# Expert weights asked for later in a spectral-mixing and top-k expert kernel

## The chip, the cores and the metric

The kernel runs on one core of one Trainium2 chip, as one launch. The metric is the device time of an execution in microseconds; the time before is 379.39 us, the median of three runs (379.3 to 380.17). All arithmetic is in float32, apart from small whole numbers in bfloat16.

## The reference

```python
# x (8, 2496, 256), filt_r, filt_i (1249, 256)
X = np.fft.rfft(x, axis=1)
y = np.fft.irfft(X * (filt_r + 1j * filt_i)[None], n=2496, axis=1)     # gfnet mixing
# y as x (19968, 256); w_gate (256, 8), w1 (8, 256, 1024), w2 (8, 1024, 256), capacity 80
logits = x @ w_gate
expert_idx = np.argmax(logits, axis=1)
gate_w = softmax(logits)[np.arange(N), expert_idx]
out = np.zeros((N, D))
for e in range(8):
    tok_idx = np.where(expert_idx == e)[0]
    if len(tok_idx) > capacity:                 # the 80 tokens with the largest gate_w
        tok_idx = tok_idx[np.argpartition(-gate_w[tok_idx], capacity)[:capacity]]
    h = np.maximum(x[tok_idx] @ w1[e], 0.0)
    out[tok_idx] = gate_w[tok_idx, None] * (h @ w2[e])
```

So of 19968 mixed tokens only 640 (80 for each of 8 experts) go through an expert. All other rows of the output are zero.

## The kernel before, in words

The forward transform and the filter are done for all 8 batches as small matrix products (80 steps of the main loop, up to about 238 us). The result stays in the frequency domain: per batch a "page" of 128 x 5120 numbers, written to the DRAM tensors `yf` (the last batch stays in SBUF as `yt`). Gate values of all tokens come from a narrow inverse transform, and VectorE picks the 80 tokens for each expert by thresholds.

Only the rows of picked tokens are transformed back. For that the rows of the inverse transform's table that belong to the picked tokens are gathered by GpSimd (`gather_rows`, an indirect DMA into `gt`), turned by VectorE (`turn_rows`, into `wt`), and multiplied with the batch's page on TensorE (`fill(n)`: the next n of 20 steps of a round). There are 7 rounds of 128 rows, in the code 0 to 6 and in this text first to seventh or last. The first four rounds take one batch each; the last three take four groups of 32 rows from batches 4 to 7. At a round's end ScalarE copies the result into `yr` (one buffer; the sixth round's goes into `z`), and SyncE writes it to the DRAM tensor `y_sel`.

Then come the experts (`experts`). For each, 80 rows of `y_sel` are gathered by GpSimd with an indirect DMA, turned on TensorE (`turn`, tile `px`), and go through two layers (`layer1`, tile `ph`; `layer2`, tile `po`). Results are scattered to the output. The first two experts' rows, `xg_first`, are gathered from the first six rounds alone, and the last round's share is added on TensorE straight from `yr`. The gathers `xg_True` of the other six read all of `y_sel`, so they wait for the last row write too. On TensorE the order is: turn 0 and 1, layer 1 of the first and the second expert, layer 2 of the first with the turn of the third expert in its middle, layer 1 of the third, and so on.

An expert's weights are 2 MB, asked for by `load_weights(e)` as two DMAs of 1 MB each from SyncE's queue into a tile of 128 x 4096. Eight experts share five places: an own buffer (`weights`), and four buffers of pages, once the page's last reader is through. Which expert gets which place is the table `WT`. The order of everything here is that of the code (a manual schedule): each engine works off its instructions in the order of the program, and an instruction of SyncE that waits for a buffer keeps back all the later ones. SyncE's DMAs use eight completion counters in turn, so that each waits for the DMA eight places before it.

Of the kernel before, what the change touches and what calls it, by code (L numbers as in the profile page):

```python
# [13 lines left out]
F32 = mybir.dt.float32  # L14
# [5 lines left out]
B, S, C = 8, 2496, 256  # L20
# [13 lines left out]
E, FF = 8, 1024  # L34
NDB, NFC = C // 128, FF // 128
# [3 lines left out]
NH = 2  # L39
# [58 lines left out]
def kernel(  # L98
# [11 lines left out]
    nc = tc.nc  # L110
# [148 lines left out]
    with tc.manual_schedule():  # L259
        keep = pool("keep", 1)  # L260
        late = pool("late", 1)
        sp = pool("pick", 1)
        gt_p = pool("gt", 4)
        u_p = pool("u", 2)
# [565 lines left out]
        def load_page(b, where, tag="page", mark=None, eng=nc.sync):  # L830
            pages[b] = where.tile([128, NS * C], F32, name=f"page_{b}", tag=tag)
            if mark is not None:
                mark(pages[b][:, 0:1], 0.0)
            flat = yf[b].rearrange("p k i s w -> p (k i s w)")
            m = NS * C // 4
            for i in range(4):
                eng.dma_start(out=pages[b][:, m * i:m * i + m], in_=flat[:, m * i:m * i + m])
# [27 lines left out]
        where = {u: (r, c) for r, us in enumerate(ROUNDS) for c, u in enumerate(us)}  # L865

        def fill(n):
            for _ in range(n):
                r, s = todo.pop(0)
                if s == 0:  # L870
                    st["po"] = fps.tile([128, C], F32, name=f"pr_{r}", tag="f")
                w = 128 if r < EARLY else 32
                for c in range(0, 128, w):
                    b = ROUNDS[r][c // 32][0]
                    nc.tensor.matmul(st["po"][c:c + w, :], lhsT=wts[r][:, s, c:c + w],  # L875
                                     rhs=yt_t[:, :, s] if b == B - 1 else columns(pages[b], s), start=(s == 0),
                                     stop=(s == NS - 1))
                if s == NS - 1:
                    yr = (zs[:].rearrange("p e s -> p (e s)") if r == NR - 2 else
                          yr_p.tile([128, C], F32, name=f"yr_{r}", tag="yr"))  # L880
                    nc.scalar.copy(out=yr[:], in_=st["po"][:])  # L881
                    nc.sync.dma_start(
                        out=y_sel[128 * r:128 * r + 128, :], in_=yr[:])
                    st["yr"] = yr
# [6 lines left out]
        for g in range(NG):  # L891
            filter_in(g)
            nc.sync.dma_start(out=d_t[:, 4 * g:4 * g + 4, :],
                              in_=d_dram.ap()[:, 4 * g:4 * g + 4, :])
# [102 lines left out]
        for k in range(NK):  # L997
# [35 lines left out]
            if 75 <= k < 79:  # L1033
                nc.scalar.copy(out=st["u1"][:, k - 75],
                               in_=zero_t[:, 0:1].unsqueeze(2).to_broadcast([128, NS, 32]))
# [8 lines left out]
        def turn_all(r, units=None):  # L1044
            for b, g in ROUNDS[r][slice(*units) if units else slice(None)]:
                turn_rows(b, g)

        for name in ("t2", "pr", "fwd"):
# [6 lines left out]
        ones_f = near_p.tile([cap, 128], F32, name="ones_f")  # L1055
        nc.vector.memset(ones_f[:], 1.0)
        WT = [(w_p, "w"), (last, "page"), (late, "page0"), (pg_p, "page"), (late, "page1"),
              (w_p, "w"), (last, "page"), (late, "page0")]
        ws = {}

        def load_weights(e):
            where, tag = WT[e]
            ws[e] = where.tile([128, NDB * FF + NFC * C], F32, name=f"w_{e}", tag=tag)
            nc.sync.dma_start(out=ws[e][:, 0:NDB * FF].rearrange("p (k f) -> p k f", k=NDB),
                              in_=moe_w1[e].rearrange("(k p) f -> p k f", p=128))
            nc.sync.dma_start(out=ws[e][:, NDB * FF:].rearrange("p (k d) -> p k d", k=NFC),
                              in_=moe_w2[e].rearrange("(k p) d -> p k d", p=128))

        load_page(2, late, "page1", nc.vector.memset)
        load_page(3, last)  # L1070
        load_weights(0)
        for g in range(3):
            t = gt2_p.tile([128, NS, 32], F32, name=f"gt_z_{g}", tag="gt")
            nc.gpsimd.memset(t[:], 0.0)
# [32 lines left out]
        kept, rcnt, cnt = mark(B)  # L1107
        fill(13)
        load_page(5, pg_p)
        load_weights(1)  # L1110
        turn_last(7)
        turn_last(8)
        st["poff"] = poff = ranks(B, cnt)
# [11 lines left out]
        row_index(EARLY, B)  # L1125
        gather_all(4)
        fill(10)
        load_page(6, late, "page1", eng=nc.gpsimd)
        turn_all(3, (3, 4))
        for b, g in ROUNDS[5][:3]:  # L1130
            gather_rows(b, g)
        pos = faults(None, None, None)
        slots(f_t)
        fill(20)
        turn_all(4)
        for b, g in ROUNDS[5][3:] + ROUNDS[6][:3]:
            gather_rows(b, g)
        weights_of(cc)
        fill(20)
        load_weights(2)  # L1140
        turn_all(5)
        gather_rows(*ROUNDS[6][3])
# [11 lines left out]
        for e in range(NH):  # L1154
            nc.gpsimd.indirect_dma_start(
                out=xg[e][:], out_offset=None, in_=y_sel[0:128 * (NR - 1), :],
                in_offset=bass.IndirectOffsetOnAxis(ap=idxg[:, e:e + 1], axis=0),
                bounds_check=128 * (NR - 1) - 1, oob_is_err=False)
        fill(20)
        for e in (3, 4):  # L1160
            load_weights(e)
        assert not todo and not zeros

    def finish(names):
# [10 lines left out]
    def experts(fp, psF, load, first):  # L1175
# [25 lines left out]
            nc.vector.tensor_copy(out=xss[e][:], in_=px[:, :, 0:cap])  # L1201

        def layer1(e, between=None):
            w1 = ws[e][:, 0:NDB * FF].rearrange("p (k f) -> p k f", k=NDB)
            xs = xss.pop(e)
            hT = fp.tile([128, NFC, cap], F32, name=f"hT_{first}_{e}", tag="hT")
            for m in range(2):
                if m and between:
                    between()
                ph = psF.tile([128, 4, 128], F32, name=f"ph_{first}_{e}_{m}", tag="ph", bufs=3)  # L1210
                for i in range(4):
                    for k in range(NDB):
                        for c in (0, 64):
                            f = 512 * m + 128 * i + c
                            nc.tensor.matmul(ph[c:c + 64, i, 0:cap], lhsT=w1[:, k, f:f + 64],  # L1215
                                             rhs=xs[:, k, :], start=(k == 0),
                                             stop=(k == NDB - 1))
                if m == 0:
                    nc.scalar.activation(out=hT[:, 0:4, :], in_=ph[:, :, 0:cap], func=AF.Relu)
                else:  # L1220
                    nc.vector.tensor_scalar(out=hT[:, 4:8, :], in0=ph[:, :, 0:cap],
                                            scalar1=0.0, scalar2=None, op0=AL.max)
            hTs[e] = hT

        def layer2(e, mid=None):
            w2 = ws[e][:, NDB * FF:].rearrange("p (k d) -> p k d", k=NFC)
            hT = hTs.pop(e)
            if e < E - 1:
                po = psF.tile([128, NDB, 128], F32, name=f"po_{first}_{e}", tag="po")
                for d in range(NDB):  # L1230
                    if d == 1 and mid:
                        mid()
                    for fc in range(NFC):
                        for c in (0, 64):
                            nc.tensor.matmul(  # L1235
                                po[c:c + 64, d, 0:cap],
                                lhsT=w2[:, fc, 128 * d + c:128 * d + c + 64], rhs=hT[:, fc, :],
                                start=(fc == 0), stop=(fc == NFC - 1))
                yTs[e] = fp.tile([128, NDB, cap], F32, name=f"yT_{first}_{e}", tag="yT")
                nc.vector.tensor_copy(out=yTs[e][:], in_=po[:, :, 0:cap])  # L1240
                return
            po = psF.tile([128, C], F32, name=f"po_{first}_{e}", tag="po")
            for fc in range(NFC):
                nc.tensor.matmul(po[0:cap, :], lhsT=hT[:, fc, :], rhs=w2[:, fc, :],
                                 start=(fc == 0), stop=(fc == NFC - 1))
            put(e, po)
# [26 lines left out]
        for e in range(E):  # L1273
            if e == E - 2:
                layer2(e, mid=lambda: back(e - 1))
                layer1(e + 1, between=lambda: back(e))
                layer2(e + 1)
                break
            if e + 1 < E:
                layer1(e + 1)  # L1280
            if e > 0:
                back(e - 1)
            if e + 2 < E and not (first and e == 0):
                turn(e + 2)
            if first and e + 4 < E:
                gather(e + 4)
            if first and e == 0:
                layer2(e, mid=lambda: turn(2))
            else:
                layer2(e)  # L1290
            n = e + 5 if first else e + 3
            if n < E:
                load(n)

# [9 lines left out]
    def general(tc, gctx):  # L1304
# [61 lines left out]
        wpool = gctx.enter_context(tc.tile_pool(name="weights2", bufs=3))  # L1366

        def load(e):
            ws[e] = wpool.tile([128, NDB * FF + NFC * C], F32, name=f"w2_{e}", tag="w")
            nc.sync.dma_start(out=ws[e][:, 0:NDB * FF].rearrange("p (k f) -> p k f", k=NDB),  # L1370
                              in_=moe_w1[e].rearrange("(k p) f -> p k f", p=128))
            nc.sync.dma_start(out=ws[e][:, NDB * FF:].rearrange("p (k d) -> p k d", k=NFC),
                              in_=moe_w2[e].rearrange("(k p) d -> p k d", p=128))

        experts(fp, psF, load, False)
# [412 lines left out]
```

## Time and profile before

| what | us |
|---|---|
| median of three runs | 379.39 |
| the profiled execution | 379.92 |
| its span, first to last instruction | 378.1 |
| TensorE busy | 351.0 |
| VectorE, GpSimd, ScalarE busy | 240.1, 181.3, 132.8 |
| DMA bytes | 109.92 MB, mean 291 GB/s |

In the rows of the profile, PE is TensorE's products, PEld its loading of the stationary operand, DVE VectorE, ACT ScalarE, POOL GpSimd and SPq SyncE's queue. A row of the timeline gives the start, the length, the engine, the line of the kernel, the operation and its tiles, how many, and in brackets the idle time before it with what ended it. A row of the waits gives who waited for whom, the total, how often and the longest. In the rows of the DMA queues, q1 is SyncE's queue, q0 GpSimd's, q8 and q14 fetch instructions; they give packets, MB and the share of the 16 DMA engines' time. "GB/s" rows cut the asked stretch into 40 slices.

### The profile page before, as it was taken

The numbers are of one execution on the slowest core, as the hardware profiler recorded it, in microseconds if no ns is written. First come the engines' busy times: TensorE is split into PE (matmuls) and PEld (weight loads), VectorE is DVE, ScalarE is ACT, GpSimd is POOL, SyncE is SP. The second block draws the span as 40 slices with busy tenths as digits, with TensorE's granted clock in tenths as the row PEclk, the third lists the DMA queues.
The fourth block names the chain that finished last, engine by engine and source line by source line (L and its number), as shares of the span: only waits on it lengthen the run. The fifth ranks groups of instructions, "written<-read, shape, count | busy, mean of one in ns | idle before, by whom it ended". The sixth has DMA issues, their size and how long they took to land. (4 is left out here: it accounts for less than half of the span.)

```text
span 378.1 us, 9670 instructions
## 1 busy us (share of the span) xinstructions
PE 351.0 (93%) x3941; PEld 311.2 (82%) x3941; DVE 240.1 (63%) x494; ACT 132.8 (35%) x275; POOL 181.3 (48%) x250
## 2 busy tenths in 40 slices
PE   8888999999999999999999998998897989897990
PEld 4788989989989899899899897697784756786880
DVE  6049666757868858879989889769959540111110
ACT  1545545454545454454444465140100000010110
POOL 8337555544655536636457858850085102223120
PEclk9999999999999999999999999999999999999997
DMA  7998699979988999989989999799999773999310
GB/s 220 287 324 275 190 341 291 341 253 316 344 257 291 332 317 309 372 235 285 353 286 279 395 298 341 261 404 392 413 398 408 272 248 70 346 366 368 106 33 12
DMA packets 41099, 109.92 MB, mean 291 GB/s; under 512 B 4202, under 2 KB 14312, under 8 KB 39176
## 3 DMA queue, kind: packets, MB, share of 16 engines
q1 hardware_dynamic: 36534, 95.94, 74.7%
q0 software_dynamic: 4240, 13.15, 9.6%
q8 instruction: 33, 0.54, 0.6%
q10 hardware_dynamic: 274, 0.14, 0.2%
q14 instruction: 18, 0.15, 0.1%
HBM read 70.42 MB, written 40.37 MB: 293 GB/s over the span
## 5 line engine op out<-in xcount | busy, mean ns | idle before, releaser
L359 POOL TENSOR_TENSOR yt<-p 128x256 f32<-128x256 f32 x156 | 113.3, 748 | 89.7 <-DVE p L351 86.4
L351 DVE TENSOR_TENSOR p<-pb,ft 128x1024 f32<-128x1024 f32 x80 | 96.9, 1214 | 39.2 <-issue 17.9
L316 PE MATMUL pa<-wf_t,x 117*128 117x120 f32 x704 | 90.5, 275 | 2.5 <-DMA x<-in_x_dram 2.5
L316 PEld LDWEIGHTS pa<-wf_t,x 117*128 117x128 f32 x704 | 84.6, 192 | 3.7 <-issue 1.9
L341 PE MATMUL pb<-d_t,t 128*128 128x128 f32 x640 | 84.7, 275 | 1.7 <-ACT t L334 1.7
L341 PEld LDWEIGHTS pb<-d_t,t 128*128 128x128 f32 x640 | 77.7, 192 | 2.2 <-ACT t L334 2.2
L321 ACT COPY tt<-pa 128x480 f32<-128x480 f32 x96 | 47.8, 515 | 78.2 <-PE pa L316 76.0
L875 PE MATMUL pr<-page,wt 128*32 128x256 f32 (+1 forms) x520 | 63.9, 380 | 2.1 <-issue 2.1
L875 PEld LDWEIGHTS pr<-page,wt 128*32 128x32 f32 (+1 forms) x520 | 46.1, 134 | 15.7 <-issue 3.8
L334 ACT COPY t<-pt 128x512 f32<-128x512 f32 x80 | 47.2, 589 | 15.6 <-PE pt L330 13.8
L330 PE MATMUL pt<-ident,tt 128*128 128x128 f32 x320 | 48.6, 274 | 0.4 <-ACT tt L321 0.4
L372 DVE STREAM_TRANSPOSE u<-yt 128x512 f32<-128x512 f32 x70 | 48.9, 699 | 0.0
L852 POOL DMA_INDIRECT gt<-rows_tbl,idxr x28 | 29.4, 1052 | 33.7 <-DVE idxr L694 19.0
L330 PEld LDWEIGHTS pt<-ident,tt 128*128 128x128 f32 x320 | 37.2, 142 | 1.9 <-issue 1.2
L863 DVE STREAM_TRANSPOSE wt<-gt 128x640 f32<-128x640 f32 x28 | 22.4, 827 | 8.2 <-DMA gt<-rows_tbl,idxr 8.1
L1215 PE MATMUL ph_True<-xs_True,w 128*64 128x80 f32 x512 | 20.7, 234 | 1.5 <-issue 1.5
L395 PE MATMUL pz<-yt,wg 128*32 128x512 f32 (+1 forms) x256 | 21.7, 436 | 0.4 <-POOL yt L359 0.4
L1171 POOL DMA_INDIRECT out_dram<-ys_True,idxs x7 | 6.5, 933 | 31.7 <-ACT ys_True L1260 31.7
L1235 PE MATMUL po_True<-hT_True,w 128*64 128x80 f32 x448 | 18.3, 235 | 3.5 <-issue 3.5
L1215 PEld LDWEIGHTS ph_True<-xs_True,w 128*64 128x64 f32 x512 | 19.2, 137 | 2.4 <-issue 2.3
L881 ACT COPY yr<-pr 128x256 f32<-128x256 f32 x6 | 2.3, 379 | 53.6 <-DMA y_sel<-yr 38.4
L1235 PEld LDWEIGHTS po_True<-hT_True,w 128*64 128x64 f32 x448 | 16.6, 137 | 4.7 <-issue 4.2
(226 smaller groups left out, 287.6 us busy)
## 6 DMA issues: line engine op xcount, KB each, us to landing
out_dram<-zero_t SPq DMA_DIRECT2D x32, 624.0 KB
yf<-u SPq DMA_DIRECT2D x56, 320.0 KB
w<-in_moe_w_dram SPq DMA_DIRECT2D x16, 1024.0 KB
page<-yf SPq DMA_DIRECT2D x24, 640.0 KB
x<-in_x_dram SPq DMA_DIRECT2D x16, 936.0 KB
x<-in_x_dram SPq DMA_DIRECT2D x7, 702.0 KB
page<-yf POOLq DMA_DIRECT2D x4, 640.0 KB
fst<-in_filt_r_dram SPq DMA_DIRECT2D x10, 128.0 KB
```

The costliest lines, as they stand in the source:

```text
L316: nc.tensor.matmul(out=ps[:, j, :], rhs=wf_t, start=True, stop=True, lhsT=xt[3 * b + ch][:, j0 + j - JC * ch, 128 * cb:128 * cb + 128])
L321: nc.scalar.copy(out=tt[h][:, :, H3 * j0:H3 * j0 + hn * jn].rearrange("p s (j h) -> p s j h", h=hn), in_=v)
L330: nc.tensor.transpose(ps[:, i, :], tt[h][:, 2 * s:2 * s + 2, :].rearrange("p r n -> p (r n)"), ident[:])
L334: nc.scalar.copy(out=t2[k][:], in_=ps[:])
L341: nc.tensor.matmul(out=ps[:, :, i, :], lhsT=t[:, i, :], rhs=d_t[:, SG * g + i, :], start=True, stop=True)
L351: nc.vector.tensor_tensor(out=p[:], in1=f.unsqueeze(2).to_broadcast(shape), op=AL.mult, in0=ps[:].rearrange("p r s q -> p r (s q)").unsque ...
L359: eng.tensor_tensor(out=y[:, :, 2 * r:2 * r + 2, :], in0=a, in1=b, op=op)
L372: nc.vector.transpose(uu[h][:, :, SG * g:SG * g + SG, :].rearrange("p a s w -> p s a w"), spectrum(h)[:, SG * g:SG * g + SG])
L852: nc.gpsimd.indirect_dma_start(out=gts[b, g][:].rearrange("p s q -> p (s q)"), out_offset=None, in_=quarters, in_offset=bass.IndirectOffse ...
L875: nc.tensor.matmul(st["po"][c:c + w, :], lhsT=wts[r][:, s, c:c + w], rhs=yt_t[:, :, s] if b == B - 1 else columns(pages[b], s), start=(s = ...
L1215: nc.tensor.matmul(ph[c:c + 64, i, 0:cap], lhsT=w1[:, k, f:f + 64], rhs=xs[:, k, :], start=(k == 0), stop=(k == NDB - 1))
L1235: nc.tensor.matmul(po[c:c + 64, d, 0:cap], lhsT=w2[:, fc, 128 * d + c:128 * d + c + 64], rhs=hT[:, fc, :], start=(fc == 0), stop=(fc == NF ...
```

## The change

Five things are moved:

- the first expert's weights, asked for before the gathers of the third round, are asked for after the fourth round; the second's, asked for after the second round, go with the third's, after the fifth round;
- the fourth expert's go ahead of the last round's row write, and are held until the second of the first gathered rows has landed: ScalarE copies one element of `xg_first` of the second expert into each half of the weights' tile, and the two DMAs wait for those copies;
- the sixth expert's go into the two buffers of turned rows (tag `u`), half and half, directly after the fifth's;
- the seventh's and eighth's take the buffers of the first's and second's, after those experts;
- the seventh page (`load_page(6, ...)`) is asked for by SyncE and no longer by GpSimd.

```diff
         WT = [(w_p, "w"), (last, "page"), (late, "page0"), (pg_p, "page"), (late, "page1"),
-              (w_p, "w"), (last, "page"), (late, "page0")]
+              None, (w_p, "w"), (last, "page")]
...
-        def load_weights(e):
-            where, tag = WT[e]
-            ws[e] = where.tile([128, NDB * FF + NFC * C], F32, name=f"w_{e}", tag=tag)
-            nc.sync.dma_start(out=ws[e][:, 0:NDB * FF].rearrange("p (k f) -> p k f", k=NDB),
+        def load_weights(e, behind=None):
+            if WT[e] is None:
+                ws[e] = [u_p.tile([128, NDB * FF], F32, name=f"w_{e}_{i}", tag="u")[:]
+                         for i in range(2)]
+            else:
+                where, tag = WT[e]
+                w = where.tile([128, NDB * FF + NFC * C], F32, name=f"w_{e}", tag=tag)
+                ws[e] = w[:, 0:NDB * FF], w[:, NDB * FF:]
+            if behind is not None:
+                for part in ws[e]:
+                    nc.scalar.copy(out=part[0:1, 0:1], in_=behind)
+            nc.sync.dma_start(out=ws[e][0].rearrange("p (k f) -> p k f", k=NDB),
...
         load_page(3, last)
-        load_weights(0)
...
         load_page(5, pg_p)
-        load_weights(1)
...
-        load_page(6, late, "page1", eng=nc.gpsimd)
+        load_page(6, late, "page1")
...
         slots(f_t)
         fill(20)
+        load_weights(0)
         turn_all(4)
...
         fill(20)
+        load_weights(1)
         load_weights(2)
...
+        load_weights(3, xg[NH - 1][0:1, 0:1])
         fill(20)
-        for e in (3, 4):
-            load_weights(e)
+        load_weights(4)
+        load_weights(5)
...
-            n = e + 5 if first else e + 3
+            n = e + 6 if first else e + 3
             if n < E:
                 load(n)
```

In the lists below a row is one instruction of the engine, with its line, the tile it writes and what it reads; `w_3` is the fourth expert's weights, `yr_2` the third round's rows, `z` the sixth round's. SyncE, from the first row write to the sixth, before:

```order
L882 DMA y_sel_153<-yr_0_3103 128x256
L837 DMA page_4_3106<-yf_4_149 128x1280 x4
L882 DMA y_sel_153<-yr_1_3228 128x256
L837 DMA page_5_3231<-yf_5_150 128x1280 x4
L1064 DMA w_1_3236<-in_moe_w1_dram 128x2x1024
L1066 DMA w_1_3236<-in_moe_w2_dram 128x8x256
L882 DMA y_sel_153<-yr_2_3404 128x256
L882 DMA y_sel_153<-yr_3_3458 128x256
L882 DMA y_sel_153<-yr_4_3588 128x256
L1064 DMA w_2_3591<-in_moe_w1_dram 128x2x1024
L1066 DMA w_2_3591<-in_moe_w2_dram 128x8x256
```

and now:

```order
L837 DMA page_5_3228<-yf_5_150 128x1280 x4
L882 DMA y_sel_153<-yr_2_3398 128x256
L837 DMA page_6_3401<-yf_6_151 128x1280 x4
L882 DMA y_sel_153<-yr_3_3452 128x256
L1072 DMA w_0_3455<-in_moe_w1_dram 128x2x1024
L1074 DMA w_0_3455<-in_moe_w2_dram 128x8x256
L882 DMA y_sel_153<-yr_4_3585 128x256
L1072 DMA w_1_3588<-in_moe_w1_dram 128x2x1024
L1074 DMA w_1_3588<-in_moe_w2_dram 128x8x256
L1072 DMA w_2_3591<-in_moe_w1_dram 128x2x1024
L1074 DMA w_2_3591<-in_moe_w2_dram 128x8x256
```

The third round's rows no longer stand behind the second expert's weights, the seventh page has come in, and three experts' weights, with one row write between, now stand ahead of the sixth round's write. SyncE, from there to the experts, before:

```order
L882 DMA y_sel_153<-z_155 128x256
L882 DMA y_sel_153<-yr_6_3844 128x256
L1064 DMA w_3_3847<-in_moe_w1_dram 128x2x1024
L1066 DMA w_3_3847<-in_moe_w2_dram 128x8x256
L1064 DMA w_4_3850<-in_moe_w1_dram 128x2x1024
L1066 DMA w_4_3850<-in_moe_w2_dram 128x8x256
```

and now:

```order
L1072 DMA w_3_3763<-in_moe_w1_dram 128x2x1024
L1074 DMA w_3_3763<-in_moe_w2_dram 128x8x256
L882 DMA y_sel_153<-yr_6_3849 128x256
L1072 DMA w_4_3852<-in_moe_w1_dram 128x2x1024
L1074 DMA w_4_3852<-in_moe_w2_dram 128x8x256
L1072 DMA w_5_0_3855<-in_moe_w1_dram 128x2x1024
L1074 DMA w_5_1_3856<-in_moe_w2_dram 128x8x256
```

The fourth expert's two DMAs have moved ahead of the last round's row write, and the sixth expert's have come in behind the fifth's. ScalarE at the same place, before:

```order
L881 COPY yr_3_3458<-pr_3_3437 128x256
L881 COPY yr_4_3588<-pr_4_3507 128x256
L881 COPY z_155<-pr_5_3653 128x256
L881 COPY yr_6_3844<-pr_6_3763 128x256
L1219 ACTIVATE hT_True_0_3888<-ph_True_0_0_3889 128x320
```

and now:

```order
L881 COPY yr_3_3452<-pr_3_3431 128x256
L881 COPY yr_4_3585<-pr_4_3504 128x256
L881 COPY z_155<-pr_5_3653 128x256
L1071 COPY w_3_3763<-xg_first_1_3754 1x1 x2
L881 COPY yr_6_3849<-pr_6_3768 128x256
```

The two copies of one element stand between the sixth round's row copy and the last one's.

More of the change, by code (lines that the diff above doesn't have):

```diff
@@ L1057 @@
         WT = [(w_p, "w"), (last, "page"), (late, "page0"), (pg_p, "page"), (late, "page1"),
-              (w_p, "w"), (last, "page"), (late, "page0")]
+              None, (w_p, "w"), (last, "page")]
         ws = {}
-        def load_weights(e):
-            where, tag = WT[e]
-            ws[e] = where.tile([128, NDB * FF + NFC * C], F32, name=f"w_{e}", tag=tag)
-            nc.sync.dma_start(out=ws[e][:, 0:NDB * FF].rearrange("p (k f) -> p k f", k=NDB),
+        def load_weights(e, behind=None):
[10 more added lines that the diff above has]
+            nc.sync.dma_start(out=ws[e][0].rearrange("p (k f) -> p k f", k=NDB),
                               in_=moe_w1[e].rearrange("(k p) f -> p k f", p=128))
-            nc.sync.dma_start(out=ws[e][:, NDB * FF:].rearrange("p (k d) -> p k d", k=NFC),
+            nc.sync.dma_start(out=ws[e][1].rearrange("p (k d) -> p k d", k=NFC),
                               in_=moe_w2[e].rearrange("(k p) d -> p k d", p=128))
@@ L1203, in layer1 @@
         def layer1(e, between=None):
-            w1 = ws[e][:, 0:NDB * FF].rearrange("p (k f) -> p k f", k=NDB)
+            w1 = ws[e][0].rearrange("p (k f) -> p k f", k=NDB)
             xs = xss.pop(e)
@@ L1225, in layer2 @@
         def layer2(e, mid=None):
-            w2 = ws[e][:, NDB * FF:].rearrange("p (k d) -> p k d", k=NFC)
+            w2 = ws[e][1].rearrange("p (k d) -> p k d", k=NFC)
             hT = hTs.pop(e)
@@ L1368, in load @@
         def load(e):
-            ws[e] = wpool.tile([128, NDB * FF + NFC * C], F32, name=f"w2_{e}", tag="w")
-            nc.sync.dma_start(out=ws[e][:, 0:NDB * FF].rearrange("p (k f) -> p k f", k=NDB),
+            w = wpool.tile([128, NDB * FF + NFC * C], F32, name=f"w2_{e}", tag="w")
+            ws[e] = w[:, 0:NDB * FF], w[:, NDB * FF:]
+            nc.sync.dma_start(out=ws[e][0].rearrange("p (k f) -> p k f", k=NDB),
                               in_=moe_w1[e].rearrange("(k p) f -> p k f", p=128))
-            nc.sync.dma_start(out=ws[e][:, NDB * FF:].rearrange("p (k d) -> p k d", k=NFC),
+            nc.sync.dma_start(out=ws[e][1].rearrange("p (k d) -> p k d", k=NFC),
                               in_=moe_w2[e].rearrange("(k p) d -> p k d", p=128))
```

## The prediction

> **What bounds the kernel now.** I read the page first, then the waits of TensorE, then its timeline over the last 65 us, and from there backwards what SyncE, ScalarE, GpSimd and the DMA queues do in the same stretch.
>
> ```profile
> span 378.1 us, 9670 instructions
> PE 351.0 (93%) x3941; PEld 311.2 (82%) x3941; DVE 240.1 (63%) x494; ACT 132.8 (35%) x275; POOL 181.3 (48%) x250
> PE po_True L1235 <- issue: 3.5, 4, 1.5
> PE pr L875 <- issue: 2.1, 3, 1.0
> PE ph_True L1215 <- issue: 1.5, 5, 0.4
> ```
>
> TensorE is busy for 351.0 of 378.1 us and is the bound; the other engines matter where they make it wait. Of its waits in the second half, none is on a weight load. The largest are 7.1 us of "issue", where the profile shows nothing that it waited for: 3.5 + 1.5 in the experts, 2.1 in the round of row products before them. The busy time by stretch tells when the transfers press:
>
> ```profile
> 280.00:290.00 10.00, 9.02 (x78) 6.28 (x76) 8.31 (x17) 0.00 (x0) 7.87 (x10) 1.00 1.01 403
> 300.00:310.00 10.00, 8.94 (x157) 5.32 (x153) 6.27 (x26) 1.12 (x3) 0.00 (x0) 1.00 0.51 179
> 310.00:320.00 10.00, 9.82 (x166) 6.35 (x159) 0.33 (x1) 0.37 (x1) 1.91 (x2) 1.00 0.36 118
> 340.00:350.00 10.00, 7.51 (x195) 7.07 (x192) 1.40 (x4) 0.91 (x2) 3.61 (x4) 1.00 1.05 366
> 350.00:360.00 10.00, 9.40 (x241) 8.95 (x238) 1.83 (x5) 1.81 (x4) 1.86 (x2) 1.00 0.28 94
> ```
>
> The last three numbers are granted clock, DMA share and GB/s. The clock is 1.00 throughout. DMA is full to 300, half idle from 300 to 320, full from 320 to 350, then nearly idle. TensorE loses most (7.51 of 10) where it is full, and runs the same expert code at 9.40 once it is not. So there are two prizes, some 2 us of gaps at 288 to 291 and some 5 us in the experts, and a hole in DMA use between 300 and 320 into which the first weights could go.
>
> ```profile
> 297.73 0.80 PE L747 MATMUL pe_s<-eval,eplc 128*80 128x56 bf16 x16
> 318.67 0.45 PE L1195 MATMUL px_True<-lhot,yr 128*128 128x80 f32 x2 [0.18 <-ACT yr L881]
> 319.40 0.39 PE L1193 MATMUL px_True<-ident,xg_first 80*128 80x80 f32 x2
> 320.38 2.57 PE L1215 MATMUL ph_True<-xs_True,w 128*64 128x80 f32 x66
> 328.42 0.36 PE L1198 MATMUL px_True<-ident,xg_True 80*128 80x80 f32 x2
> 332.43 0.30 PE L1198 MATMUL px_True<-ident,xg_True 80*128 80x80 f32 x2
> 341.70 0.78 PE L1235 MATMUL po_True<-hT_True,w 128*64 128x80 f32 x17 [1.02 <-issue]
> 348.32 0.98 PE L1235 MATMUL po_True<-hT_True,w 128*64 128x80 f32 x22 [1.47 <-issue]
> 354.06 1.19 PE L1235 MATMUL po_True<-hT_True,w 128*64 128x80 f32 x28 [0.59 <-issue]
> ```
>
> The fifth round of row products ends at 297.73, the experts' first weights are used from 320.38. The other dates are those of gathered rows: the second expert's gathered rows at 319.40, the third's (first L1198) at 328.42, the fourth's at 332.43. The third's date turns out to be the tight one.
>
> ```profile
> 244.13 0.40 SPq L1064 DMA_DIRECT2D w<-in_moe_w_dram  x1
> 285.73 0.38 SPq L1064 DMA_DIRECT2D w<-in_moe_w_dram  x1
> 286.73 17.92 SPq L882 DMA_DIRECT2D y_sel<-yr  x3
> 304.74 0.39 SPq L1064 DMA_DIRECT2D w<-in_moe_w_dram  x1
> 309.96 0.34 SPq L882 DMA_DIRECT2D y_sel<-z  x1
> 318.64 0.33 SPq L882 DMA_DIRECT2D y_sel<-yr  x1
> 319.06 0.39 SPq L1064 DMA_DIRECT2D w<-in_moe_w_dram  x1
> 301.68 0.37 ACT L881 COPY yr<-pr 128x256 f32<-128x256 f32 x1 [24.17 <-DMA y_sel<-yr]
> 318.24 0.37 ACT L881 COPY yr<-pr 128x256 f32<-128x256 f32 x1 [8.30 <-PE pr L875]
> 314.92 0.96 POOL L1155 DMA_INDIRECT xg_first<-y_sel,idxg  x1 [17.46 <-DMA y_sel<-z]
> 316.19 0.95 POOL L1155 DMA_INDIRECT xg_first<-y_sel,idxg  x1 [0.30 <-issue]
> 321.15 0.94 POOL L1182 DMA_INDIRECT xg_True<-y_sel,idxg  x1 [4.01 <-PE px_True L1195]
> ```
>
> Two readings. First, a row write behind a weight load on SyncE's queue lands after that load: the write at 286.73 came just behind the second expert's weights (285.73), and ScalarE's next row copy waited for it until 301.68, about 15 us. Second, with nothing ahead of it such a write is quick: the last round's rows went out at 318.64 and the third expert's gather, which reads all of y_sel, started at 321.15, at most 2.5 us later. That gather could use those rows so soon only because the write stands ahead of the fourth expert's weights (319.06).
>
> **The change part by part.**
>
> *First expert's weights from 244 to about 287, second's and third's to about 298.* Same six DMAs, same bytes; nothing on TensorE changes. Until 286 it takes 2.1 MB out of a full DMA, so pages and gathered rows come some 5 us sooner; no TensorE wait before 288 is on them, so 0. SyncE no longer stands before the second expert's weights until the fourth round is done (285.73), so the 24.17 us of ScalarE go; what TensorE waited for there is nothing either, 0. The first three experts' weights are used from 320.38 on and would all be there by about 310: at 367 GB/s (the row of 330 to 350 below) 4.2 MB take 11.4 us from 298.5. The gaps of 2.1 us at 288 to 291 are bounded by 0 and 2.1 gain. DMA is still full there, with page seven, gathers and now the first weights where the second's were; I take 0, since the load at that place is the same.
>
> *Seventh page by SyncE.* Its four issues leave GpSimd's queue, so the gathers behind them start sooner; they feed transposes for which TensorE does not wait. 0. On SyncE the four stand behind the third round's row write, which no longer waits behind the second expert's weights; TensorE uses the page in the last two rounds, after 297.73, some 15 us later. 0.
>
> *Sixth expert's weights in the buffers of turned rows.* They go out with the fifth's, just before the experts, in place of behind the first expert. DMA was full from 320 to 350 anyway, with five loads, and is again with five. 0 by itself.
>
> *Fourth expert's weights behind the first gathered rows.* This adds two copies of one element on ScalarE, and puts the load's two DMAs on SyncE ahead of the last round's row write. Here is the cost. The rows of the transfers, one or two each for the stretches 317.5 to 319 (GB/s in 40 slices), 318.5 to 327.2, 321 to 325 (two rows), 325 to 327 and 330 to 350:
>
> ```profile
> GB/s 0 0 0 0 0 0 0 0 0 465 28 109 465 55 301 137 28 27 82 82 28 27 27 0 0 0 0 0 0 0 0 0 0 0 0 0 0 0 0 0
> q1 hardware_dynamic: 1393, 2.23, 83.8%
> DMA packets 662, 1.35 MB, mean 338 GB/s; under 512 B 16, under 2 KB 437, under 8 KB 662
> q1 hardware_dynamic: 662, 1.35, 92.8%
> q0 software_dynamic: 46, 0.08, 12.2%
> DMA packets 4621, 7.33 MB, mean 367 GB/s; under 512 B 176, under 2 KB 3731, under 8 KB 4616
> ```
>
> From 318.5 to 327.2 SyncE's queue moved 2.23 MB, the row write (0.13) and one expert's weights (2.10): a weight load issued at 319.06 is through 8.1 us later. The third expert's gather, issued at 321.15, has no packet up to 325 (all 662 are SyncE's) and its 0.08 MB run between 325 and 327: about 5.3 us, plus about 0.9 to land. The same gather with DMA idle (316.19) has its last packets in the 23rd of the 40 slices, 318.4, and is used at 319.40: at most 3.2 us in all.
>
> Step by step, in times of the trace before. The write of the sixth round (309.96) has the second and third experts' weights ahead of it, which end at about 310; it lands between 312.5 (unqueued, 2.5 us) and 314.9 (as now), say 313.0. The second gather starts 1.3 us later, 314.3, and has landed at 317.4. Two copies, below 0.37 us each (ScalarE's row copy), release SyncE at 317.7; ScalarE's own row copy at 318.24 is then not held up, between 0 and 1 us. The weights are through 7.8 us later (less the gather that shared the 8.1), 325.5; the row write behind them adds 0.36 us of data and 1 us to land: the third expert's gather starts at 326.9 instead of 321.15. With 6.2 us for it, TensorE has the rows at 333.1 instead of 328.42: a wait of 4.7 us. Its ends: with the earliest dates and a gather of 3.2 us, 328.6, hardly any wait; with the latest and the 7.3 us that the row of 328.42 allows, 8 us. I take the middle, because five weight loads are queued behind and the row under load is the nearest. Behind it on TensorE all stands still; the gathers of the fourth and fifth experts follow 1.3 us apart and are in time, since TensorE is late too.
>
> What comes back: the DMA load ends at about 351 instead of 352, while TensorE is 4.7 us later. The place of the 1.47 us gap falls on 351.5, that of 0.59 on 358, after the drain, so 0.59 and about 0.9 go: 1.5 us.
>
> Sum: 4.7 - 1.5 = +3.2 us. The profiled execution took 379.92 us (span 378.1 and 1.8 around it); the median shown is 379.39. So 379.39 + 3.2 = 382.6.
>
> The Trainium skill ("DMA: Bandwidth & Descriptors", section "Queues, rings and completion order") states that each DMA engine takes turns between the queues that have work, a packet at a time. By it a gather should be served beside the weights, not 4 us after its issue; the trace here, no packet of it before 325, does not agree.
>
> **The rivals.**
> - *Gathers served in turn.* If the third expert's gather takes 3.2 us, as when DMA is idle, the rows are there at 330.1, the wait is 1.7 and the net 1.7 - 1.5 = +0.2: 379.6. Speaking for it: only three gathers show the slow form, all behind fresh weight loads. Against: their first packets. The Trainium skill's rule above would give this.
> - *The row write isn't held, and the gaps go.* If the gathered rows come before about 316 and the weights flow at the full rate of 400 GB/s seen before 290, the row write lands by about 323.5 and the third expert's rows by 328.4: no wait. Then 0.6 to 1.5 us of the late gaps and perhaps the 2.1 us at 288 go: 377.4. It decides when the write lands before 322. Against it: 8.1 us for one load, and 2.2 us for a gather even unloaded.
> - *ScalarE's queue blocks too.* If the sixth round's rows land as late as now (314.92), the two small copies wait until about 319.4, the last row copy with them, TensorE starts the experts 1 us later, and the weights and the write shift by 2: about +5, 384.5. It decides when the second gather lands after 318.
>
> **How the numbers follow.** Held write, as summed: 0.53, at 382.6, from 380.6 to 384.6. Blocked ScalarE too: 0.09. Gathers in turn: 0.14. Not held: 0.24. A run of three varies by some 0.3%, 1.1 us, which is the bound used here for a change. So slower 0.62, same 0.14, faster 0.24. The range reaches from the middle of the not-held case, 378.0, to beyond the blocked one, 385.2.
>
> **What would show it.** Right: TensorE waits for a DMA before the first L1198 group of the experts, 2 to 7 us, its releaser the gathered rows; the last row write is issued after 318 and the third expert's gather starts at 325 or later; no issue gap after 352; no ScalarE wait of 24 us. Wrong: that gather starts before 323, or the wait is under 1 us; or gaps at 288 to 291 are gone and everything after stands 2 us earlier. What would make it wrong most simply is a row write that overtakes the weights, or rows of the sixth round that land before 312.

## The result and the profile after

The changed kernel takes 383.05 us (median of five, 382.49 to 387.19) against 379.52 (379.3 to 380.32) for the kernel before, measured beside it: a ratio of 1.012 [1.0082, 1.0158], 3.5 us slower. Measured again later, both kernels unchanged, on the chip called the third below, it was 386.25 against 380.13: 1.0157 [1.0126, 1.0187]. The profiled execution of the changed kernel is the longest of its five, 387.19 us, so its trace shows where the time goes, while its sizes are on the high side.

First the head of the page and the waits of TensorE in the changed kernel (who waited for what, total us, how often, longest):

```profile
span 385.3 us, 9670 instructions
PE 352.9 (92%) x3941; PEld 313.8 (81%) x3941; DVE 241.5 (63%) x494; ACT 133.2 (35%) x277; POOL 178.0 (46%) x246
...
PE px_True L1207 <- DMA xg_True<-y_sel,idxg: 6.3, 1, 6.3
```

TensorE's work is what it was (352.9 us, 351.0 before). There are waits for gathered rows that the kernel before does not have at all: 6.3 us ahead of the third expert's turn (L1207, which was L1198), and a smaller one ahead of the first. Next the queues and TensorE from the sixth round's end, in the changed kernel:

```profile
294.38 0.80 PE L747 MATMUL pe_s<-eval,eplc 128*80 128x56 bf16 x16
307.32 0.34 SPq L882 DMA_DIRECT2D y_sel<-z  x1
314.98 0.97 POOL L1163 DMA_INDIRECT xg_first<-y_sel,idxg  x1 [17.94 <-DMA y_sel<-z]
318.80 0.28 ACT L1071 COPY w<-xg_first 1x1 f32<-1x1 f32 x2 [11.51 <-DMA xg_first<-y_sel,idxg]
318.99 0.36 ACT L881 COPY yr<-pr 128x256 f32<-128x256 f32 x1
319.02 0.38 SPq L1072 DMA_DIRECT2D w<-in_moe_w_dram  x1
320.00 0.53 SPq L882 DMA_DIRECT2D y_sel<-yr  x1
328.38 0.94 POOL L1191 DMA_INDIRECT xg_True<-y_sel,idxg  x1 [11.18 <-DMA y_sel<-yr]
317.70 0.42 PE L1202 MATMUL px_True<-ident,xg_first 80*128 80x80 f32 x2 [2.24 <-DMA xg_first<-y_sel,idxg]
319.40 0.45 PE L1204 MATMUL px_True<-lhot,yr 128*128 128x80 f32 x2 [1.28 <-ACT yr L881]
334.72 0.53 PE L1207 MATMUL px_True<-ident,xg_True 80*128 80x80 f32 x2 [6.26 <-DMA xg_True<-y_sel,idxg]
341.43 0.42 PE L1260 MATMUL pb_True<-ident,yT_True 128*80 128x128 f32 x2
355.87 0.98 PE L1244 MATMUL po_True<-hT_True,w 128*64 128x80 f32 x22 [2.16 <-issue]
```

Read it as a chain. The sixth round's rows go out at 307.32 behind two loads, and the gather that needs them starts at 314.98, 7.7 us later. The two small copies wait for it until 318.80; the last row copy stands behind them on ScalarE (318.99, for which TensorE waits 1.28 us), the fourth expert's weights behind them on SyncE (319.02), the last row write behind those (320.00). The third expert's gather starts 8.4 us after that write, at 328.38, and its rows are there at 334.72.

```profile
320.52:323.92 3.40, 3.40 (x40) 3.26 (x41) 0.46 (x2) 0.00 (x0) 0.00 (x0) 0.50 0.88 333
323.92:330.74 6.82, 4.54 (x130) 4.38 (x126) 0.98 (x2) 0.87 (x2) 1.89 (x2) 1.00 1.05 381
330.76:340.98 10.22, 6.26 (x90) 6.09 (x92) 0.65 (x2) 0.44 (x1) 0.95 (x1) 0.50 1.05 342
340.00:350.00 10.00, 10.00 (x250) 9.64 (x250) 2.13 (x6) 1.63 (x4) 3.83 (x4) 0.95 1.00 335
```

The busy time by stretch shows what the forecast had no term for: the granted clock (third number from the right) is 0.50 for 3.4 us behind the first waits and for 10.2 us in and behind the long one, where it was 1.00 before. From 340 to 350 TensorE is busy for 10.00 of 10 us with the DMA engines still full.

### The profile page after: what moved, and what is told of

It is laid out like the page before. It is cut to its first block, busy times and chain, and to the rows that moved or that the text cites. A ratio compares the mean times of both kernels' runs of the same rounds, so it can differ in the third digit from the quotient of the medians.

```text
span 385.3 us, 9670 instructions
## 1 busy us (share of the span) xinstructions
PE 352.9 (92%) x3941; PEld 313.8 (81%) x3941; DVE 241.5 (63%) x494; ACT 133.2 (35%) x277; POOL 178.0 (46%) x246
## 5 line engine op out<-in xcount | busy, mean ns | idle before, releaser
L1224 PE MATMUL ph_True<-xs_True,w 128*64 128x80 f32 x512 | 22.1, 252 | 0.0
L395 PE MATMUL pz<-yt,wg 128*32 128x128 f32 (+1 forms) x256 | 21.7, 436 | 0.4 <-POOL yt L359 0.4
L1224 PEld LDWEIGHTS ph_True<-xs_True,w 128*64 128x64 f32 x512 | 21.3, 154 | 0.3 <-issue 0.2
L395 PEld LDWEIGHTS pz<-yt,wg 128*32 128x32 f32 x256 | 8.8, 109 | 12.3 <-issue 7.0
```

Of the source, the lines that this page charges most:

```text
L395: nc.tensor.matmul(out=ps[32 * j:32 * j + 32].rearrange("p (s w) -> p s w", s=pn), lhsT=wg[:, cb, :], rhs=yt_t[:, (2 * b + cb) % 2, 5 * j ...
```

## The experiments

**One part undone or done alone.** The first four ran on one chip, where the kernel before took 379.27 us. In the first, the fourth expert's weights follow the last row write, without the two copies; all else is as in the changed kernel:

```diff
-        load_weights(3, xg[NH - 1][0:1, 0:1])
         fill(20)
+        load_weights(3)
         load_weights(4)
```

> The changed kernel with one part undone: the fourth expert's weights go out behind the last round's row write again, without the two small copies. Held-write theory: the last row write lands about 2.5 us after its issue, the third expert's gather starts by 323 (328.4 in the changed kernel), the wait of 6.3 us before its turn falls under 1 us, TensorE's clock stays at 1.00 from 320 to 340, and the time is 376.5 to 379, 4 to 6.5 us under the changed kernel. Rival, gathers are slow because more weights are queued, whatever the order: the gather starts early but its rows still come after 330, wait over 3 us, 381 to 383. Rival, the loss is at the first gathered rows (2.2 and 1.3 us of waits before the first two turns): the wait of 6.3 us may go but the time stays within 2 us of the changed kernel.

Measured: 379.86 us (four runs, 374.96 to 381.25; too few and too far apart for an interval), above the 376.5 to 379 expected. In the third, the kernel before gets that one edit and no other (with the two copies in `load_weights`, as in the changed kernel):

```diff
...
+        load_weights(3, xg[NH - 1][0:1, 0:1])
         fill(20)
-        for e in (3, 4):
-            load_weights(e)
+        load_weights(4)
```

> The kernel before with that one part alone: the fourth expert's weights ahead of the last row write, held by two small copies behind the second gathered rows; the first three experts' weights, the seventh page and the sixth's buffers as before. Held-write theory: a wait of 4 to 6.5 us before the third expert's turn, the gather starts after 326, time 382.5 to 386, since nothing is won at 288. Rival, the loss needs the fuller queue (first three experts' weights later, fifth's and sixth's together): wait under 2 us, 379 to 381.

Measured: 385.7 us, 1.0185 [1.0102, 1.0267]. The last row write and the third expert's gather of the first kernel, then the dates of the second and its wait:

```profile
315.23 0.34 SPq L882 DMA_DIRECT2D y_sel<-yr  x1
317.78 0.94 POOL L1191 DMA_INDIRECT xg_True<-y_sel,idxg  x1 [1.84 <-PE px_True L1204]
```

```profile
293.47 0.80 PE L747 MATMUL pe_s<-eval,eplc 128*80 128x56 bf16 x16
319.58 0.53 SPq L882 DMA_DIRECT2D y_sel<-yr  x1
327.88 0.94 POOL L1185 DMA_INDIRECT xg_True<-y_sel,idxg  x1 [11.07 <-PE ph_True L1218]
334.11 0.53 PE L1201 MATMUL px_True<-ident,xg_True 80*128 80x80 f32 x2 [4.49 <-DMA xg_True<-y_sel,idxg]
```

With the weights behind the write, the gather starts at most 2.6 us after it and TensorE does not wait for it, though it still waits 3.0 us for the first gathered rows and the clock is 0.50 from 320.0 to 323.4; with the weights ahead, the gather starts 8.3 us after the write, and the loss is there without any other part of the change. So this part makes the loss. The 293.47 is told of further down.

**Is it the queue or the load?** The last row write, in the fourth kernel the last two, leaves SyncE's queue for ScalarE's:

```diff
-                    nc.sync.dma_start(
+                    (nc.scalar if r == NR - 1 else nc.sync).dma_start(
```

> The changed kernel, with the last round's row write alone issued from ScalarE's queue instead of SyncE's, the order of all else kept (the fourth expert's weights still go out first). Held-write theory, by SyncE's own queue order: the write no longer stands behind 2 MB in one queue, lands within 2.5 to 4.5 us, the third expert's gather starts at 322 to 324.5, the wait before its turn falls from 6.3 to 0 to 2.5 us, time 377.5 to 380.5. Rival, the DMA engines serve transfers in the order of issue whatever the queue: nothing moves, wait 5 to 7 us, 382 to 384.

> The changed kernel with the last two row writes (sixth and last round) issued from ScalarE's queue. Held-write theory for both: the sixth round's rows no longer stand behind the second and third experts' weights, so the first gathers start at about 310 to 312 instead of 315, the waits of 2.2 and 1.3 us before the first two turns go, and the fourth expert's weights start earlier, by 315.5; the wait before the third turn is 0 to 1 us; time 374.5 to 377.5, under both kernels. Rival, order of issue whatever the queue: first gathers at 314 to 315, 381 to 384. Rival, the gain at 288 to 291 is not real: 378 to 380 with all waits gone.

Measured: 380.8 us, 1.0059 [1.0027, 1.0091], with `r == NR - 1`; 380.83, 1.0058 [1.0024, 1.0091], with `r >= NR - 2`. The last write in the first of them with the two halves of the fourth expert's weights, and the sixth round's write and first gather in the second:

```profile
317.35 0.38 SPq L1072 DMA_DIRECT2D w<-in_moe_w_dram  x1
317.82 0.42 SPq L1074 DMA_DIRECT2D w<-in_moe_w_dram  x1
317.71 0.40 ACTq L882 DMA_DIRECT2D y_sel<-yr  x1
323.78 0.94 POOL L1191 DMA_INDIRECT xg_True<-y_sel,idxg  x1 [8.23 <-PE ph_True L1224]
```

```profile
307.03 0.33 ACTq L882 DMA_DIRECT2D y_sel<-z  x1
313.68 0.96 POOL L1163 DMA_INDIRECT xg_first<-y_sel,idxg  x1 [16.92 <-issue]
```

From the last write to the gather it is now 6.1 us in place of 8.4. But the write has also moved in time: it goes out at 317.71, between the two halves of the load, with 1 MB ahead of it and no longer 2. At the 367 GB/s of the prediction's row a megabyte takes 2.9 us, an estimate that covers all of the 2.3 us won, so nothing here shows that the other queue itself helps. For the sixth round, with both loads still ahead, it is 6.7 us in place of the 7.2 and 7.7 of the first kernel above and of the one with the last write alone moved, whose sixth write stands in SyncE's queue (306.55 to 313.72 and 305.61 to 313.33); the same order took 5.9 on the third chip. So the place in SyncE's queue is the smaller part at most: a row write that stands behind a bulk load is slow from either queue, and the rival of service in the order of issue is not excluded. My expectation of 374.5 to 377.5 us for the second was wrong for this reason; the first came out just above its range, with a wait of 2.8 us.

**The first gathers.** Their delay, too, can be taken away. On a second chip (before: 380.29 us) the first expert's weights went back to the place of the kernel before, the second's to after the fourth round, the third's to after the fifth, with the fourth's behind the last row write as above:

```diff
         load_page(3, last)
+        load_weights(0)
...
-        load_weights(0)
+        load_weights(1)
...
-        load_weights(1)
         load_weights(2)
...
```

> The fourth expert's weights behind the last row write (as in the first experiment), and the first expert's weights again asked for before the third round's gathers, the second's after the fourth round, the third's after the fifth. If the 2.2 and 1.3 us before the first two turns come from 4 MB of weights ahead of the sixth round's write: with 2 MB ahead, issued about 295 and through by 302, that write lands within 3 us of its issue, the first gathers start at 309 to 311, both waits are under 0.3 us, the clock stays at 1.00, and the time is 2.5 to 4 us under the first experiment and 2 to 3 us under the kernel before. If the gaps at 288 to 291 went because the first expert's weights left the DMA before 286, they are back (1.5 to 2.5 us), and the time is that of the kernel before, within 1 us. If they went because SyncE no longer stands before the second expert's weights, they stay away.

Measured: 379.07 us, 0.9966 [0.9937, 0.9994], the lowest median of all kernels here, though by less than the 2 to 3 us I expected. One more kernel left the first expert's weights late, kept the fourth's behind the last row write, and put the third's behind the sixth round's write (`load_weights(2)` after the `fill(10)` that ends that round):

> The first experiment's kernel with the third expert's weights moved behind the sixth round's row write. Write held by queued weights: that write lands within 3 us and the first gathers start at 309.5 to 311 instead of 313.7; but they now run beside the third expert's weights, so they take 5 to 6 us instead of 3, land at 314 to 316.5, and a wait of 0 to 1.5 us is left before the first two turns (3.0 in the first experiment). Time 1 to 3 us under it. Rival, first gathers late for another reason (GpSimd, or the write's own latency): start still at 313 or later.

Measured: 379.66, 0.9979 [0.9951, 1.0007], not told from the kernel before. The writes and first gathers of the two, one after the other, and the wait that the second still has:

```profile
310.65 0.34 SPq L882 DMA_DIRECT2D y_sel<-z  x1
313.32 0.96 POOL L1163 DMA_INDIRECT xg_first<-y_sel,idxg  x1 [14.49 <-DMA y_sel<-z]
```

```profile
308.40 0.34 SPq L882 DMA_DIRECT2D y_sel<-z  x1
311.00 0.97 POOL L1163 DMA_INDIRECT xg_first<-y_sel,idxg  x1 [14.15 <-issue]
318.62 0.42 PE L1202 MATMUL px_True<-ident,xg_first 80*128 80x80 f32 x2 [1.93 <-DMA xg_first<-y_sel,idxg]
```

With nothing just ahead, write to gather takes 2.6 to 2.7 us. But the weights that now follow the write lie before the gather itself, 311.00 to 318.62, and TensorE waits for it, 1.9 us where I expected at most 1.5: the collision has moved by one transfer.

**Parts that I had priced at 0.** On the same chip, the version of 379.07 us with the seventh page left to GpSimd (`load_page(6, late, "page1", eng=nc.gpsimd)`), and the kernel before with the second expert's weights moved to after the fourth round and nothing else:

> As the one beside it (first expert's weights early, second's after the fourth round), but the seventh page by GpSimd's queue as in the kernel before. If the page's place in GpSimd's queue made the gaps at 288 to 291 (it stands ahead of the gathers of the last two rounds), they come back, 1.5 to 2.5 us, and the gathers behind it end some 2 us later; if not, both kernels have the same time within 0.5 us.

> The kernel before with a single edit: the second expert's weights asked for after the fourth round and no longer after the second, so that SyncE does not stand before them from 271 to 286. If that standing is what the rest of the change repairs: ScalarE's wait of 24 us goes, the gaps at 288 to 291 go or shrink below 0.5 us, time 1.5 to 3 us under the kernel before. If the gaps come from the load on the DMA at that place alone: no change within 0.5 us.

Measured: 380.35 us, 1.0003 [0.9977, 1.003], and 379.85, 1.001 [0.9978, 1.0041]. Neither is told from the kernel before. Set beside the version of 379.07 us itself, twelve runs of each, the one with GpSimd's page is 1.3 us slower [0.5, 2.2], more than the 0.5 us within which I expected them to agree; no row of the two profiles shows where. ScalarE's long wait is gone in the latter kernel, from 24.17 us to 13.67, with another releaser, while the gaps near 288 stay at 2.1 us, with the clock at 0.50 behind them from 291.9 to 295.3, and TensorE gains nothing.

**Do the gaps near 288 belong to the change?** In the profiles shown they stand before (2.1 us) and not after, and the fifth round ends at 294.38 instead of 297.73. But the kernel before with the fourth expert's weights moved, whose order is that of the kernel before up to 300, has no such gap and ended it at 293.47. So both kernels, unchanged, and the changed one with the first expert's weights put back, ran on a third chip:

```diff
         load_page(3, last)
+        load_weights(0)
...
         fill(20)
-        load_weights(0)
         turn_all(4)
```

> The kernel before, unchanged, for its profile beside the three others on one chip: in the runs so far the issue gaps of 2 us near 288 (the L875 group) stand in some profiles and not in others, though two kernels with the same order up to that place differ in it. Theory (the gaps are of the execution or the chip, not of the change): this profile and that of the changed kernel, on the same chip, both have them or both lack them, each within 0.5 us. Rival (the first expert's weights leaving that stretch removes them): 1.5 to 2.1 us here, under 0.5 us in the changed kernel. Time by both: the ratio is 1.000, 379 to 380 us.

> The changed kernel, unchanged, on the same chip. Both theories: 382.5 to 383.5 us, TensorE waits 4 to 6.5 us for the third expert's gathered rows. Theory (gaps of the execution): the fifth round ends within 1 us of where it ends in the kernel before on this chip. Rival (the moved first weights bring the round forward): it ends 2 to 3.5 us earlier than there, with no gap near 288.

> The changed kernel with the first expert's weights alone put back to where the kernel before asks for them (before the first gathers of pages). Theory (moving them was worth nothing): 382.5 to 383.5 us, as the changed kernel; the fifth round ends at the same time; the write of the sixth round has one load less shortly ahead of it, so the two first gathers may come up to 1 us sooner, which could take up to 1 us off. Rival (the move brings 2 to 3 us by the gaps near 288): 385 to 386 us.

Measured: 379.23 us, 386.25 and 386.06; ratios 0.9976 [0.9951, 1.0001], 1.0157 [1.0126, 1.0187] and 1.015 [1.0114, 1.0187]. The second is some 3 us above what either view expected; the third lies at the rival's number, but it has to be compared with the 386.25 beside it, and by that the move is worth nothing that can be told. The waits near 288 and the fifth round's end, of the first two in this order:

```profile
PE pr L875 <- issue: 2.0, 4, 1.0
296.66 0.80 PE L747 MATMUL pe_s<-eval,eplc 128*80 128x56 bf16 x16
```

```profile
PE pr L875 <- issue: 1.6, 2, 1.0
296.37 0.80 PE L747 MATMUL pe_s<-eval,eplc 128*80 128x56 bf16 x16
```

With the first weights put back the gaps are 1.1 us and the round ends at 296.51. On one chip all three have the gaps and end the round within 0.3 us of each other. The other experiments agree: none of the four profiles of the first chip has such a gap between 270 and 298, and all eight of the second and third have them, 1.1 to 2.1 us, whatever the order of the loads. So the difference of 3 us between the first two profiles does not go with the change; in these experiments it goes with the chip (on which chips the first two profiles were taken is not on record). What makes the gaps is not shown.

**What the falling clock costs.** 140 matmuls of 64 columns fill the wait ahead of the third expert's turn, into a tile that the turn overwrites:

```diff
+            if first and e == 2:
+                for i in range(140):
+                    c = 64 * (i % 2)
+                    nc.tensor.matmul(px[c:c + 64, 0, 0:cap], lhsT=ws[0][0][:, c:c + 64],
+                                     rhs=ident[:, 0:cap], start=True, stop=True)
```

> The changed kernel with 140 matmuls of 64 columns on TensorE ahead of the third expert's turn, into a tile that the turn overwrites: at the 37 ns of the layer 1 matmuls they fill some 5.2 of the 6.3 us in which TensorE waits there. Nothing that is waited for changes. Theory (the wait costs 6.3 us and then about 1.8 us more, because the granted clock falls to 0.54 after it and the layer 1 behind it takes 4.13 instead of 2.38 us): the layer takes 2.4 to 2.7 us, the granted clock in 330 to 340 is over 0.85, and the time falls by 1.5 to 2 us, to 381 to 381.5. Rival (the slow layer has another cause, such as weights or instructions that arrive late while DMA is full): it still takes about 4 us and the time stays at 382.5 to 383.5, or rises if the 140 last longer than the wait.

Measured: 389.86 us, 1.0248 [1.0209, 1.0287]. I had sized the fill wrongly: 140 float32 matmuls are 280 in the records, and they outlasted the wait by some 7 us (the gather starts at 326.29, and with 6.2 us its rows would be there at 332.5; the turn comes at 339.82). What follows the turn can still be compared, first in the changed kernel, then in the filled one, on one chip:

```profile
333.96 0.53 PE L1207 MATMUL px_True<-ident,xg_True 80*128 80x80 f32 x2 [6.03 <-DMA xg_True<-y_sel,idxg]
334.42 2.40 PE L1244 MATMUL po_True<-hT_True,w 128*64 128x80 f32 x32
339.37 0.41 PE L1260 MATMUL pb_True<-ident,yT_True 128*80 128x128 f32 x2
332.00:336.00 4.00, 2.04 (x26) 1.87 (x28) 0.32 (x1) 0.00 (x0) 0.00 (x0) 0.50 1.03 336
```

```profile
339.82 0.36 PE L1212 MATMUL px_True<-ident,xg_True 80*128 80x80 f32 x2
340.10 1.33 PE L1249 MATMUL po_True<-hT_True,w 128*64 128x80 f32 x32
343.57 0.42 PE L1265 MATMUL pb_True<-ident,yT_True 128*80 128x128 f32 x2
340.00:344.00 4.00, 4.00 (x102) 3.79 (x101) 0.90 (x3) 0.44 (x1) 0.00 (x0) 1.00 0.32 78
```

From the third expert's turn to the turning back of the first one's result: 339.37 - 333.96 = 5.41 us with the clock at 0.50, 343.57 - 339.82 = 3.75 with it at 1.00. The same 32 products of layer 2 take 2.40 and 1.33. The wait thus costs 1.7 us beyond itself. The DMA engines are also emptier behind the filled wait; that the clock alone makes the difference rests on two other runs. The same stretch takes 3.76 us with full DMA and the clock at 1.00 in the kernel before (next section). In the kernel before with the fourth expert's weights moved it takes 6.2 us (334.11 to 340.33), though from 334 to 338 the DMA engines are at a share of 0.03; the clock there is 0.50 up to 339.4.

## Why the prediction was right, and where it was not

The sign and the mechanism were right: the fourth expert's weights ahead of the last row write hold it, and the third expert's gather behind it. The size agrees less well than 382.6 against 383.05 suggests; on the third chip the same change costs 6 to 7 us, outside the range given. In the first pair of profiles the part behind the fifth round's end is 10.5 us longer (90.9 us against 80.4) and the part ahead of it 3.3 us shorter, which is not the change's doing (last section but one of the experiments). That the median came so near to the sum is at least in part luck. On the third chip both kernels have the gaps near 288, so the sum can be checked there date by date. The kernel before, then the changed one (the last row of the waited turn and of the turning back stand above):

```profile
319.38 2.50 PE L1215 MATMUL ph_True<-xs_True,w 128*64 128x80 f32 x65
327.73 0.36 PE L1198 MATMUL px_True<-ident,xg_True 80*128 80x80 f32 x2
331.49 0.42 PE L1251 MATMUL pb_True<-ident,yT_True 128*80 128x128 f32 x2
365.06 3.68 PE L1244 MATMUL po_True<-w,hT_True 128*80 128x256 f32 x16
```

```profile
318.86 0.45 PE L1204 MATMUL px_True<-lhot,yr 128*128 128x80 f32 x2 [1.33 <-ACT yr L881]
320.62 6.20 PE L1224 MATMUL ph_True<-xs_True,w 128*64 128x80 f32 x128
371.40 3.68 PE L1253 MATMUL po_True<-w,hT_True 128*80 128x256 f32 x16
```

| up to | before | changed | step | predicted |
|---|---|---|---|---|
| fifth round's end | 296.66 | 296.37 | -0.3 | 0 |
| first layer 1 | 319.38 | 320.62 | +1.5 | 0 |
| third expert's turn | 327.73 | 333.96 | +5.0 | +4.7 |
| first result turned back | 331.49 | 339.37 | +1.7 | 0 |
| last layer 2 | 365.06 | 371.40 | -1.5 | -1.5 |
| sum (before rounding) | | | +6.3 | +3.2 |

- *Third expert's wait, 4.7.* Measured +5.0 here. The wait itself is 6.0, and about 1 us of it is taken back, since the issue gaps in the layers 1 before it are gone (1.8 us in the kernel before), while 3.3 us of them run at half clock. The shares were right: 9.2 us from the load's issue to the gather were summed and 9.4 measured (319.02 to 328.38), and 6.2 to 6.3 for the gather. One end of the range for this wait was added up wrongly: with the rows landing at 312.5 the sum's own steps give 326.4 for the gather and 329.6 for its rows, not 328.6; nothing else hangs on it.
- *Late gaps, -1.5.* The size came out: behind the first result's turning back, the issue gaps here add up to 3.4 us before and 2.0 now. The reason given, that they fall after the transfers, is not shown: from 340 to 350 the first profile has full DMA and no gap, and its gap of 2.16 us at 355.87 stands where the DMA share is 0.13 (355 to 360).
- *"ScalarE's own row copy at 318.24 is then not held up, between 0 and 1 us".* Wrong. The step that failed is the landing of the sixth round's rows, "say 313.0": the gather behind it started at 314.98 (314.48 on the third chip), so the copies came at 318.80 and the row copy behind them. TensorE waits 1.3 us for it in both profiles, and its step in the table is 1.5 us. This is the rival "ScalarE's queue blocks too", whose condition was met: the second gather landed after 318 (copies at 318.80, on the third chip 318.26). It had a chance of 0.09, and its 384.5 is nearer to the third chip's 386.25 than the sum.
- *The clock.* No step had it, since the trace before shows 1.00 as long as TensorE works. It adds 1.7 us here behind the long wait; in the first profile, where the same stretch takes 341.43 - 334.72 = 6.71 us, 3 us. The difference is when the clock comes back: at 337.5 here, 3.6 us after the wait, and at 341.0 there, 6.3 us after it.
- *First expert's weights, seventh page, sixth's buffers, each 0.* Right for the first (386.06 against 386.25). Open for the page: left with GpSimd it measured 1.3 us more (380.35 against 379.07, [0.5, 2.2]) in one comparison, so its move may have been worth something. The sixth's buffers were not tried alone.
- *Gathers served in turn.* Refuted: 6.2 to 6.3 us from issue to use in three profiles (328.38 to 334.72, 327.81 to 333.96 on the third chip, 327.88 to 334.11 with that part alone). In the stretch from 327.8 to 332 of the changed kernel, in which three gathers were issued, the table of the DMA queues (packets, MB, share) has only SyncE's packets and one fetch of instructions, none of GpSimd's:

```profile
q1 hardware_dynamic: 1097, 1.55, 103.9%
```

- The marks named beforehand came out: wait of 2 to 7 us at the third turn, last write after 318, gather after 325, no 24 us wait on ScalarE. The mark "no issue gap after 352" did not: 2.16 us at 355.87 in the first profile, though only gaps of 0.4 or less on the third chip. The mark of being wrong, gaps at 288 gone and everything after 2 us earlier, was there in the first profile and misled, as the gaps come and go without the change.

Why the first comparison gave 3.5 us and the later one 6 to 7 is not settled: its shorter executions were not profiled.

## What to carry to other kernels

A small write on which gathers wait belongs ahead of a bulk load in time, not only in its queue: behind 2 MB it cost 8.4 us, from another queue and between the two halves still 6.1, ahead of them 2.6. Price a wait of the matrix engine by what stands behind it as well, since the clock may fall and the work after it was then half as fast for 3.6 us in one execution and 6.3 in another. Before a gain between two profiles is put down to a change, look whether an unchanged kernel shows it too.

## What was not expected of the hardware

The clock falls after waits that are short. In the changed kernel on the third chip the waits before the first turns are 0.36 and 1.33 us, and 3.4 us from 320.48 on run at 0.50; with both row writes on ScalarE's queue, a single wait of 1.82 us was followed by a layer of 4.03 us in place of 2.38:

```profile
320.48:323.88 3.40, 3.40 (x51) 3.28 (x52) 0.33 (x1) 0.44 (x1) 0.00 (x0) 0.50 0.99 366
```

```profile
330.56 0.36 PE L1207 MATMUL px_True<-ident,xg_True 80*128 80x80 f32 x2 [1.82 <-DMA xg_True<-y_sel,idxg]
332.00 4.03 PE L1224 MATMUL ph_True<-xs_True,w 128*64 128x80 f32 x64
```

In the kernel with the third expert's weights behind the sixth write, the wait of 1.93 us left the clock at 1.00.

The dates at which the clock changes have a pattern. In the changed kernel's first profile it falls and comes back at 320.5, 323.9, 330.8 and 341.0, which are 3.4, 6.8 and 10.2 us apart; on the third chip it does at 320.5, 323.9, 330.7 and 337.5, 3.4, 6.8 and 6.8 us apart. In all eight profiles in which the clock falls around these waits, the distances are 3.4 us or two or three times that. So the clock stays down for whole steps of 3.4 us, and where a wait lies between these dates is a likely reason why the same wait costs 1.7 us in one execution and 3 in another; no run here varies that alone.

The Trainium skill ("TensorE: Matmul & The Clock Gate", section "Part 1: The HAM clock gate (the "warmup" mystery)") states that the clock goes to half after at least one idle window of about 3.4 us, and that the window runs free. The halving and the distances of 3.4 us agree with these traces. That the window has to be idle does not: a wait of 1.82 us, or two of 0.36 and 1.33, came before a fall. Why the wait of 1.93 us did not bring one is not shown; it may have been cut in two by the edge of a window.
